# A fused LayerNorm, linear attention and SiLU MLP: reordered first loads, split first weights, deferred duplicate columns

## Chip, cores and metric

The kernel runs on one core of a Trainium2 chip. The metric is the device time of one execution in microseconds (us), as the median of several runs. The core has a matmul engine (PE, with its weight loads shown apart as PEld), three engines for other arithmetic (DVE, ACT and POOL), and SP, which here only issues DMA transfers. ACT issues a few transfers too.

## What is computed

The input x is 2048 rows of 448 numbers in bfloat16. There is one sequence; 16 heads of 28 columns; the MLP is 1792 wide.

```python
xn = _layernorm(x, axis=-1)
# linear attention
q, k, v = split((xn @ wqkv).reshape(B, S, 3, H, Dh))
pq, pk = q @ w_phi, k @ w_phi                     # per head, 28 x 28
phi_q = concat([softmax(pq), softmax(-pq)])
phi_k = concat([softmax(pk), softmax(-pk)])
kv, z = phi_k.T @ v, phi_k.sum(rows)
o = (phi_q @ kv) / (phi_q @ z + 1e-6)
# MLP
y = silu(xn @ w1) @ w2
return x + o @ wo + y
```

## The kernel before, in words

**Tiles and stages.** The rows are 16 tiles of 128; four tiles make a chunk. A contraction over 448 is cut in seven slices of 64, and nearly every matmul is issued as a pair (`pair`, L437 to L448): two matmuls of 64 rows each, one on the lower and one on the upper half of the array, each into its own PSUM bank. Two banks are a slot; slots 0 to 2 are taken and given in rotation (`take`, `give`), slot 3 is used by hand for transposes, for the fold of w_phi into w_qk, for the attention sums KV, and at the end for U.

**Head.** x is loaded by tile (`load_x`), w1 in blocks of 128 rows (`load_w1`, L510) and a last block of 64 (w16). PE first runs warm-up matmuls on a block of ones (`warm`, L488). LayerNorm of a tile is `LN_st` (statistics, L573), `LN_ag` (mean and variance, L577, variance plus epsilon into `ve`, L579, the inverse root on POOL, L581) and `LN_b` (the normalised tile xnd on DVE, L596 or L589). xnd is 512 wide: columns 448 to 511 repeat columns 0 to 63, so that every window of 128 columns can be transposed. For tiles 0 to 3 PE transposes it (`X_tr`, L459), and ACT and DVE copy the result to xT (`X_ev`, L464 and L631); for later tiles a DMA transposes (`X_dma`, L612). `F1ph` forms xn @ w1 for 128 or 256 rows, in two phases `ph` (which half of the array works on which bank) and by blocks b of w1; its `six` part uses the last 64 rows of w1. The functions `f1a`, the F1A and F1B loops and `c0` run it for chunk 0, as data arrives; `F1silu` writes silu to hT.

**Fold.** q @ w_phi is one product with a folded weight. w_qk's 448 rows are loaded in four parts to wraw; `FT_tr` transposes them on PE (L459, copies at L867), and `FM` multiplies by BD, a block diagonal of w_phi, into wqk (copies at L886). `V` forms values, `QK` scores and their exponentials; DVE sums them (L706), POOL scales (L713), a DMA transposes (phT). `F2_early` forms hT @ w2 of tiles 0 to 7 into Ye, while `KV` sums phi_k.T @ v.

**Tail.** For tiles 8 to 15 `ph0` and `ph1` form hT @ w2 in a slot seeded with x by ACT. `U(t)` forms the attention output of two tiles, DVE scales it (L800, L801, L809), and a DMA transposes it to oT (L811). `WO(t)` multiplies oT by w_o for tiles 0 to 7 and DVE adds Ye (L833); `WO_two` does the same for tiles 8 to 15 on top of the slot that already holds x and the MLP. `store` sends two tiles out (L816). `nextu` calls U ahead of its use.

**Order.** `_Prog` records every operation with a planned duration and its dependencies. PE runs them in the order of recording, and so do operations marked `ordered`, on their engine. The others are ordered by a planner (`_pass`, L239), which prices each operation by a constant and DMA by `service` (L473) and picks by due time, with shaken repeats. `chained` loads (L506) are issued only when the load four places earlier in `chain` has landed. SP issues in one line: a transfer that waits holds back all that stand behind it.

Of the kernel before, what the change touches and what calls it, by code (L numbers as in the profile page):

```python
# [140 lines left out]
class _Prog:  # L141
# [97 lines left out]
    def _pass(self, when, shake=0):  # L239
# [46 lines left out]
        while done < n:  # L286
# [20 lines left out]
            if o.is_dma:  # L307
                issue_end = t + o.dur
                eng_free[o.eng] = issue_end
                if o.fixed is not None:  # L310
                    o.end = t + o.fixed
                else:
                    x0 = max(issue_end + 900.0, dma_free[0])
                    dma_free[0] = x0 + o.nbytes
                    o.end = dma_free[0] + 300.0 + o.late
# [14 lines left out]
def bass_parallel_sum__linear_kernel_hedgehog__dense_activation_silu__prompt_kernel(  # L330
# [21 lines left out]
    with es:  # L352
# [23 lines left out]
        st6 = sb("st6", [128, NT, 6], F32)  # L376
        mv = sb("mv", [128, NT, 2], F32)
        ve = sb("ve", [128, NT], F32)
# [8 lines left out]
        wsrc = hT[:, NH - 1, FT - 1, :]  # L387
        ones_bf = wsrc[:, 0:128]
# [84 lines left out]
        def service(nbytes, run):  # L473
            return nbytes / run * (12.0 + 0.0475 * run) / 16.0
# [10 lines left out]
        P.op("pool", 230, lambda e: e.memset(wsrc, 1.0), [], [wsrc], name="ones", ordered=True)  # L485
        P.op("pool", 290, lambda e: e.affine_select(ident[:], ones_bf, [[1, 128]], ALU.is_equal, 0.0, base=0,
                                                    channel_multiplier=-1), [ones_bf], [ident[:]], name="ident", ordered=True)
        def warm(n, sl=2, d=216.0):  # L488
            for i in range(n):
                pair([(bank(2 * sl + q)[:, 0:512], ones_bf[HALF[q], :], wsrc[HALF[q], :], True, True) for q in range(2)],  # L490
                     512, "warm", dur=d)

        P.unit = "warm"
        warm(10, d=427.0)


# [13 lines left out]
        def load_w1(b, eng):  # L510
            chain.append(load(w1_sb[:, 2 * b:2 * b + 2, :].rearrange("p h f -> p (h f)"), B_w1[b * 128:(b + 1) * 128, :],
                              128 * FF * 2, 2 * FF, f"w1{b}", eng=eng, issue=480))
# [4 lines left out]
        load_x(1, 2, eng="act")  # L517
        load_w1(0, "sp")
        load_w1(1, "act")
        load_x(2, 3, eng="act")  # L520
        load_w1(2, "sp")
        for q, eng in enumerate(("sp", "act")):
            chain.append(load(w1_sb[HALF[q], 6, :], B_w1[384:448, q * 896:(q + 1) * 896], 64 * 896 * 2, 1792, f"w16{q}", eng=eng,
                              issue=480))
        load_x(3, 4, eng="act")
        P.op("pool", 300, lambda e: e.memset(BD[:], 0.0), [], [BD[:]], name="bd0", ordered=True)
# [6 lines left out]
        def load_bulk():  # L533
# [6 lines left out]
            for b in range(NB):  # L540
                r = 128 if b < 3 else 64
                chained(700.0, wraw[0:r, b, 8:904], A_wqkv[b * 128:b * 128 + r, 0:896], r * 1792, 1792, f"wqk{b}", issue=450)
# [9 lines left out]
        for q in range(2):  # L552
            for l in range(2):
                p0 = (64 if q else 8) + l * DH
                load(BD[p0:p0 + DH, :, l * DH:(l + 1) * DH], wpv[q, l], DH * NB * DH * 2, DH * 2, f"wphi{q}{l}", issue=430)

# [4 lines left out]
        def pads_init():  # L561
            for sl in range(NE):
                pads = E[:, sl].rearrange("p k (c n) -> p (k c) n", n=64)[:, :, 56:64]
                P.op("pool", 330, lambda e, pads=pads: e.memset(pads, 0.0), [], [pads], name="pads", ordered=True)
# [5 lines left out]
        def LN_st(t, od=False):  # L570
            P.unit = f"LN{t}"
            xs = x_sb[:, t, :]
            P.op("dve", 630, lambda e: e.bn_stats(st6[:, t, :], xs), [xs], [st6[:, t, :]], name="bnst", ordered=od)  # L573

        def LN_ag(t, od=False):
            P.unit = f"LN{t}"
            P.op("dve", 180, lambda e: e.bn_aggr(mv[:, t, :], st6[:, t, :]), [st6[:, t, :]], [mv[:, t, :]], name="bnag", ordered=od)  # L577
            P.op("dve" if od else "pool", 120 if od else 220,
                 lambda e: e.tensor_scalar(ve[:, t:t + 1], mv[:, t, 1:2], EPS_LN, None, ALU.add),  # L579
                 [mv[:, t, 1:2]], [ve[:, t:t + 1]], name="ve", ordered=od)  # L580
            P.op("pool", 580, lambda e: e.tensor_tensor(rstd[:, t:t + 1], ve[:, t:t + 1], neghalf[:], ALU.pow),  # L581
                 [ve[:, t:t + 1], neghalf[:]], [rstd[:, t:t + 1]], name="rstd", ordered=od)

        def LN_b(t, parts=((0, D), (D, 512)), od=False):
# [7 lines left out]
            for a, b in parts:  # L592
                dst = xnd[:, t % NX, a:b]
                src = x_sb[:, t, 0:64] if a == D else x_sb[:, t, a:b]
                P.op("dve", 90 + 0.72 * (b - a),
# [19 lines left out]
        def X_tr(t, sl, ws):  # L615
            P.unit = f"X{t}"
            for k, w in enumerate(ws):
                tpair([(bank16(2 * sl + q)[:, k * 64:(k + 1) * 64], xnd[HALF[q], t % NX, w * 64:w * 64 + 128],
                        ident[HALF[q], q * 64:(q + 1) * 64]) for q in range(2)], 64, "xT_tr")

        def X_ev(t, sl, ws, both=False):
# [3 lines left out]
            for q in (1, 0):  # L625
                src = bank16(2 * sl + q)[:, 0:n * 64].rearrange("p (s n) -> p s n", s=n)
                dst = xT[:, 0, ws[0]:ws[-1] + 1:ws.step, j * 128 + q * 64:j * 128 + (q + 1) * 64]
                if q == 0 and not both:
# [20 lines left out]
        def X_rest():  # L649
            P.unit = "Xrest"  # L650
            ws = range(1, 4, 2)
            for t in range(2):
                for k, w in enumerate(ws):
                    tpair([(bank16(6 + q)[:, (2 * t + k) * 64:(2 * t + k + 1) * 64], xnd[HALF[q], t % NX, w * 64:w * 64 + 128],
                            ident[HALF[q], q * 64:(q + 1) * 64]) for q in range(2)], 64, "xT_tr")
            for q in range(2):
                src = bank16(6 + q)[:, 0:256].rearrange("p (t w n) -> p w t n", t=2, w=2)
                dst = xT[:, 0, 1:4:2, 0:256].rearrange("p w (t r n) -> p w t r n", t=2, r=2)[:, :, :, q]
                dve(lambda e, dst=dst, src=src: e.tensor_copy(dst, src), 66 + 46 * 4, [src], [dst], "xT_ev")
# [114 lines left out]
        def F2_ph(t, sl, ph, a, b, mid=None, at=3):  # L774
# [44 lines left out]
        def WO_mm(t, ub, sl, a, b, seeded):  # L819
            P.unit = f"WO{t}"  # L820
            for s in range(NS):
                op = pair([(bank(2 * sl + q)[:, a:b], oT[HALF[q], ub, s, :], wo_sb[HALF[q], s, a:b], (not seeded) and s == 0, s == NS - 1)
                           for q in range(2)], b - a, "wo")
                swapped(op, (2 * sl, 2 * sl + 1), 0)

        def WO(t, ub):
            sl = take()
            WO_mm(t, ub, sl, 0, D, False)
            for q in range(2):
                bk = bank(2 * sl + q)[:, 0:D]  # L830
                y = Ye[:, (t + q) % NYE, :]
# [381 lines left out]
```

## Time and profile before

| | |
|---|---|
| Median of 13 runs | 149.57 us (149.03 to 151.97) |
| Profiled execution: its own time | 149.03 us |
| Profiled execution: span from first to last instruction | 147.3 us |
| PE busy | 142.3 us |
| DVE, ACT, POOL busy | 92.2, 88.9, 76.3 us |
| Warm-up matmuls start | 1.40 us |
| First transposes of x | 5.64 us |
| First matmul with w1 | 6.42 us |
| First matmul of V(2) | 19.86 us |
| First matmul of chunk 1 (F1) | 33.41 us |
| Last WO_two starts | 142.98 us |

Times in the profile count from the first instruction. A row of the timeline gives start, duration, engine, source line, operation, output and inputs, shapes and count, and in brackets how long the engine had been idle and what ended the wait. A line can be that of a helper: L446 is every matmul pair, L459 every transpose on PE, L464 every ACT operation, L477 every load. The chain that ended last is followed backwards from the last instruction through whatever released each step.

### The profile page before, as it was taken

What the parts mean: (1) busy time and instruction counts of PE and PEld (TensorE: products, weight loads), DVE (VectorE), ACT (ScalarE), POOL (GpSimd) and SP (SyncE); (2) the same over time, 40 slices, a digit from 0 to 9 for tenths busy, and PEclk for the clock granted to TensorE, in tenths of its full rate; (3) what the DMA queues carried; (4) which work ended last, traced back from release to release, by engine and by line L of the source; (5) the groups of instructions that cost most, each with busy time, mean ns of one, the idle gap of its engine ahead of it and who ended that gap; (6) DMA issues with size and microseconds to landing.
All of it is one profiled execution on the core that took longest, in us unless ns stands there. A gap on an engine that the chain in (4) does not pass through costs nothing.

```text
span 147.3 us, 5049 instructions
## 1 busy us (share of the span) xinstructions
PE 142.3 (97%) x2188; PEld 87.6 (59%) x2188; DVE 92.2 (63%) x176; ACT 88.9 (60%) x119; POOL 76.3 (52%) x87
## 2 busy tenths in 40 slices
PE   6999999999999999999999999999999999999982
PEld 2589965554556555555555556655555555557861
DVE  1977379999986496841077997871158154457532
ACT  4248789898768785975987758598592022040401
POOL 3326025059999959899123999999970000000000
PEclk9999999999999999999999999999999999999999
DMA  5997989975920895369850051333769406224592
GB/s 131 387 264 162 289 250 260 119 156 162 181 55 6 168 176 122 89 145 166 179 116 0 0 123 24 71 80 69 85 134 92 100 4 187 67 77 120 145 141 89
DMA packets 44110, 19.11 MB, mean 130 GB/s; under 512 B 37240, under 2 KB 43448, under 8 KB 44088
## 3 DMA queue, kind: packets, MB, share of 16 engines
q1 hardware_dynamic: 43432, 17.87, 58.6%
q10 hardware_dynamic: 656, 0.92, 1.8%
q8 instruction: 17, 0.28, 0.9%
q14 instruction: 5, 0.04, 0.1%
HBM read 8.17 MB, written 1.84 MB: 68 GB/s over the span
## 4 chain that ended last, share of the span: by engine, by line
PE 93%; DMA 3%; DVE 1%; POOL 0%; issue 0%; ACT 0%; SPq 0%; POOLq 0%
PE psum L446 92%; DMA E<-E 3%; PE psum L459 1%; DVE E L809 1%; POOL hT L485 0%; DVE x_sb L843 0%; ACT xT L464 0%; POOL neghalf L484 0%; SPq L1153 0%; POOLq L1198 0%
## 5 line engine op out<-in xcount | busy, mean ns | idle before, releaser
L713 POOL TENSOR_TENSOR E<-E,Rk 128x896 bf16<-128x896 bf16 x32 | 53.3, 1700 | 7.0 <-DVE Rk L708 5.3
L446 PE MATMUL psum<-xT,w_sb 64*128 64x512 bf16 (+2 forms) x522 | 46.8, 324 | 0.3 <-ACT xT L464 0.3
L446 PE MATMUL psum<-w_sb,hT 64*128 64x448 bf16 (+1 forms) x504 | 45.3, 328 | 0.0
L446 PEld LDWEIGHTS psum<-w_sb,hT 64*128 64x128 bf16 x504 | 25.6, 94 | 16.4 <-ACT psum L464 0.2
L706 DVE TENSOR_REDUCE Sk<-E 128x64 f32<-128x1792 bf16 x16 | 31.9, 2004 | 2.9 <-ACT E L464 2.9
L464 ACT ACTIVATE hT<-psum 128x1024 bf16<-128x1024 f32 (+1 forms) x29 | 28.0, 992 | 8.8 <-PE psum L446 8.5
L446 PEld LDWEIGHTS psum<-xT,w_sb 64*128 64x128 bf16 x522 | 25.0, 94 | 13.9 <-issue 0.4
L464 ACT ACTIVATE E<-psum 128x896 bf16<-128x896 f32 x32 | 27.4, 916 | 6.4 <-PE psum L446 5.2
L446 PE MATMUL psum<-wqk,xT 64*128 64x448 bf16 x224 | 23.6, 349 | 0.0
L446 PEld LDWEIGHTS psum<-wqk,xT 64*128 64x128 bf16 x224 | 12.2, 94 | 8.6
L464 ACT ACTIVATE psum<-x_sb 128x448 f32<-128x448 bf16 (+1 forms) x10 | 4.6, 468 | 20.0 <-PE psum L446 19.4
L581 POOL TENSOR_TENSOR rstd<-ve,neghalf 128x1 f32<-128x1 f32 x16 | 9.1, 571 | 7.7 <-DVE ve L579 6.9
L765 POOL TENSOR_TENSOR Ye<-Ye,x_sb 128x448 f32<-128x448 f32 x8 | 8.2, 1038 | 8.8 <-DVE Ye L763 8.8
L446 PE MATMUL psum<-wo_sb,E 64*128 64x448 bf16 (+1 forms) x126 | 11.9, 328 | 0.5 <-DMA E<-E 0.5
L446 PE MATMUL psum<-wv_sb,xT 64*128 64x448 bf16 x112 | 12.0, 349 | 0.0
L589 DVE TENSOR_SCALAR xnd<-x_sb,mv,rstd 128x896 bf16<-128x896 bf16 x12 | 8.2, 722 | 5.9 <-POOL rstd L581 5.9
L573 DVE BATCH_NORM_STATS2 st<-x_sb 128x6 f32<-128x448 bf16 x16 | 9.5, 604 | 3.7 <-DMA x_sb<-in_A_x_dram 3.6
L763 DVE TENSOR_TENSOR Ye<-psum,Ye 128x448 f32<-128x448 f32 x8 | 5.0, 621 | 10.3 <-ACT Ye L464 10.2
L833 DVE TENSOR_TENSOR x_sb<-psum,Ye 128x448 bf16<-128x448 f32 x8 | 4.8, 606 | 9.7 <-PE psum L446 6.8
L809 DVE TENSOR_TENSOR E<-psum,rden 128x224 bf16<-128x224 f32 x32 | 10.2, 382 | 0.2
L446 PEld LDWEIGHTS psum<-wo_sb,E 64*128 64x128 bf16 x126 | 5.8, 94 | 4.3 <-DMA E<-E 0.8
L464 ACT ACTIVATE x_sb<-psum 128x448 bf16<-128x448 f32 (+1 forms) x8 | 3.9, 494 | 7.4 <-PE psum L446 7.4
(48 smaller groups left out, 101.8 us busy)
## 6 DMA issues: line engine op xcount, KB each, us to landing
w_sb<-in_B_w_dram SPq DMA_DIRECT2D x4, 448.0 KB, 5.2
out_dram<-x_sb SPq DMA_DIRECT2D x7, 224.0 KB, 2.1
w_sb<-in_B_w_dram SPq DMA_DIRECT2D x4, 336.0 KB, 5.6
x_sb<-in_A_x_dram SPq DMA_DIRECT2D x2, 448.0 KB, 4.8
wv_sb<-in_A_wqkv_dram SPq DMA_DIRECT2D x2, 392.0 KB, 5.4
wo_sb<-in_A_wo_dram SPq DMA_DIRECT2D x14, 56.0 KB, 2.3
phT<-in_A_wqkv_dram SPq DMA_DIRECT2D x3, 224.0 KB, 4.1
w_sb<-in_B_w_dram ACTq DMA_DIRECT2D x1, 448.0 KB, 4.9
```

Of the source, the lines that this page charges most:

```text
L446: ins = e.matmul(dst, lhsT, rhs, start=st, stop=sp, skip_group_check=True)
L459: ins = e.transpose(dst, src, idn)
L464: return P.op("act", d_act(n), lambda e: e.activation(dst, src, func, scale=scale), reads=reads or [src], writes=writes or [dst], table=ta ...
L573: P.op("dve", 630, lambda e: e.bn_stats(st6[:, t, :], xs), [xs], [st6[:, t, :]], name="bnst", ordered=od)
L581: P.op("pool", 580, lambda e: e.tensor_tensor(rstd[:, t:t + 1], ve[:, t:t + 1], neghalf[:], ALU.pow), [ve[:, t:t + 1], neghalf[:]], [rstd[ ...
L589: dve(lambda e: e.tensor_scalar(dst, src, mv[:, t, 0:1], rstd[:, t:t + 1], ALU.subtract, ALU.mult), 734, [src, mv[:, t, 0:1], rstd[:, t:t ...
L706: dve(lambda e: e.tensor_reduce(Sk[:, t % 3, :].rearrange("p (h g) -> p h g", g=2), Er, AXL.X, ALU.add), d_dve(1792), [Er], [Sk[:, t % 3, ...
L713: pool(lambda e, Eh=Eh, Rb=Rb: e.tensor_tensor(Eh, Eh, Rb, ALU.mult), 1770, [Eh, Rh], [Eh], "phi%d" % qk)
L763: dve(lambda e: e.tensor_tensor(y, b, y, ALU.add), d_dve(D), [b, y], [y], "ye_d")
L765: pool(lambda e: e.tensor_tensor(y, y, x_sb[:, t, :], ALU.add), 1110, [y, x_sb[:, t, :]], [y], "ye_x")
L809: dve(lambda e, dst=dst, src=src, rb=rb: e.tensor_tensor(dst, src, rb, ALU.mult), d_dve(224), [src, r], [dst], "o")
L833: dve(lambda e, bk=bk, y=y, dst=dst: e.tensor_tensor(dst, bk, y, ALU.add), d_dve(D), [bk, y], [dst], "out")
```

## The change

It is one edit of many small parts.

- **First loads.** x0 and x1 go first, both on SP. w1's first block is split: columns 0 to 511 of both halves are loaded from ACT once POOL has cleared BD, columns 512 to 895 later. x2 and x3 are one transfer on ACT. The four small w_phi loads move from SP's front to behind the four w_qk loads, waiting for the first of these.
- **LayerNorm.** The `ve` operation goes. The statistics get a third group of three values that holds epsilon, so the variance comes out with epsilon in it.
- **Warm-up.** The ones are 128 columns set by DVE, read four times over; nine pairs instead of ten.
- **Duplicates.** Columns 448 to 511 of xnd for tiles 0 and 1 are first set to zero and filled later; `X_rest` then redoes window 6, too.
- **Head order.** `six` parts come after the third block; part 6 of F1 runs on 512 columns for one silu; c0(0, 0) is two halves; tile 3's copy is in two parts; the copy of tile 1's second part is all on ACT; X_rest, FT_tr and FM use slots in rotation, and slot 3 joins the rotation until phase 0 ends. V(0) comes before FM(3) and FM(2), V(2) after. POOL's pad memsets wait for a PE mark.
- **Tail.** `WO` is seeded with Ye by ACT, and its result copied out by ACT and DVE. U(6) runs inside `F2_ph(12, ..)`, U(14) inside `WO(4)` after its fourth pair; the default place of a unit inside `F2_ph` is after pair 6 instead of 3.
- **Planner constants** for DMA.

```diff
-        P.op("pool", 230, lambda e: e.memset(wsrc, 1.0), [], [wsrc], name="ones", ordered=True)
+        P.op("dve", 100, lambda e: e.memset(ones_bf, 1.0), [], [ones_bf], name="ones", ordered=True)
...
+        zero = P.op("pool", 300, lambda e: e.memset(BD[:], 0.0), [], [BD[:]], name="bd0", ordered=True)
+        P.op("pool", 100, lambda e: e.memset(xnd[:, 0:2, D:512], 0.0), [], [xnd[:, 0:2, D:512]], name="xz", ordered=True)
+        P.op("dve", 90, lambda e: e.memset(st6[:, :, 6:9], 0.0), [], [st6[:, :, 6:9]], name="eps0", ordered=True)
+        P.op("dve", 90, lambda e: e.memset(st6[:, :, 8:9], D * EPS_LN), [], [st6[:, :, 8:9]], name="eps", ordered=True)
-        warm(10, d=427.0)
+        warm(9, d=427.0)
...
         load_x(0, 1)
-        load_x(1, 2, eng="act")
-        load_w1(0, "sp")
-        load_w1(1, "act")
-        load_x(2, 3, eng="act")
-        load_w1(2, "sp")
+        load_x(1, 2)
+        load_w1(0, 0, 512, "act", after=zero)
+        load_w1(1, 0, 896, "sp")
+        load_x(2, 4, eng="act")
+        load_w1(2, 0, 896, "sp")
+        load_w1(0, 512, 384, "act")
...
-        load_x(3, 4, eng="act")
...
+            for q in range(2):
+                for l in range(2):
+                    p0 = (64 if q else 8) + l * DH
+                    load(BD[p0:p0 + DH, :, l * DH:(l + 1) * DH], wpv[q, l], DH * NB * DH * 2, DH * 2, f"wphi{q}{l}", issue=430,
+                         after=chain[-4]).late = 2500.0
...
-            P.op("dve" if od else "pool", 120 if od else 220,
-                 lambda e: e.tensor_scalar(ve[:, t:t + 1], mv[:, t, 1:2], EPS_LN, None, ALU.add),
-                 [mv[:, t, 1:2]], [ve[:, t:t + 1]], name="ve", ordered=od)
...
-        LN_b(0, ((0, 256), (256, D), (D, 512)), True)
+        LN_b(0, ((0, 256), (256, D)), True)
...
+        for t in range(2):
+            LN_b(t, ((D, 512),))
...
+        for name, k in (("U0", 0), ("X3", 0), ("U1", 1), ("A", 1), ("60", 0), ("B", 0), ("X", 1), ("61", 0), ("T0", 0),
+                            ("01", 0), ("20", 0), ("M0", 0), ("21", 0), ("40", 1), ("M1", 0), ("T1", 0), ("41", 0), ("V0", 0),
+                            ("M3", 1), ("M2", 0), ("V2", 0)):
+            if k:
+                free.insert(0, free.pop(k))
+            head[name]()
...
+            for q in range(2):
+                act(bank(2 * sl + q)[:, 0:D], Ye[:, (t + q) % NYE, :], ACTF.Identity, D, name="seed")
+            WO_mm(t, ub, sl, 0, D, mid)
...
-                dve(lambda e, bk=bk, y=y, dst=dst: e.tensor_tensor(dst, bk, y, ALU.add), d_dve(D), [bk, y], [dst], "out")
+                if q:
+                    dve(lambda e, bk=bk, dst=dst: e.tensor_copy(dst, bk), d_dve(D), [bk], [dst], "out")
+                else:
+                    act(dst, bk, ACTF.Identity, D, name="out")
...
-        ph1(12, 0, D)
-        nextu(6)
+        F2_ph(12, sls[12, 0], 1, 0, D, lambda: nextu(6), 8)
         ph0(14, 0, M)
-        wo2(4, 12)
+        WO(4, ub[4], lambda: nextu(14))
+        WO_two(12, ub[12], sls[12, 0], 0, D)
```

In the list of the head, U0 and U1 are the two phases of part 6 of F1 on tiles 0 and 1, 60 and 61 those on tiles 2 and 3, X3 the transposes of tile 3, A and B the halves of c0(0, 0), X is X_rest, T0 and T1 are FT_tr, M0 to M3 FM, V0 and V2 the values, and the other pairs of digits c0(part, phase).

## The prediction, on record before the result

> **What bounds the kernel now.** I read the page's busy times and its chain first, then the waits of the matmul engine (PE), then the timeline at the three places where PE stops.
>
> ```profile
> span 147.3 us, 5049 instructions
> PE 142.3 (97%) x2188; PEld 87.6 (59%) x2188; DVE 92.2 (63%) x176; ACT 88.9 (60%) x119; POOL 76.3 (52%) x87
> ...
> PE 93%; DMA 3%; DVE 1%; POOL 0%; issue 0%; ACT 0%; SPq 0%; POOLq 0%
> ```
>
> ```profile
> engine line waited for: us in total, times, longest us
> PE psum L446 <- POOL hT L485: 1.4, 1, 1.4
> PE psum L446 <- DMA E<-E: 0.5, 1, 0.5
> PE psum L446 <- ACT xT L464: 0.3, 1, 0.3
> ```
>
> PE is the bound and hardly waits: only the stretch before its first useful matmul, one short wait behind it, and one 0.5 us wait near the end can be won. Its rows run at one pitch, so moving matmuls about inside the stream is worth nothing. The head, from the timeline:
>
> ```profile
> 1.40 4.45 PE L446 MATMUL psum<-hT 64*128 64x512 bf16 x20 [1.40 <-POOL hT L485]
> ...
> 3.85 0.18 DVE L577 BATCH_NORM_AGGREGATE mv<-st 128x2 f32<-128x6 f32 x1
> 4.06 0.15 DVE L579 TENSOR_SCALAR ve<-mv 128x1 f32<-128x1 f32 x1
> 4.13 0.62 DVE L573 BATCH_NORM_STATS2 st<-x_sb 128x6 f32<-128x448 bf16 x1
> ...
> 5.07 0.79 DVE L596 TENSOR_SCALAR xnd<-x_sb,mv,rstd 128x256 bf16<-128x256 bf16 x3
> ...
> 5.64 0.52 PE L459 MATMUL psum<-ident,xnd 64*128 64x64 bf16 x10
> ...
> 6.42 0.55 PE L446 MATMUL psum<-xT,w_sb 64*128 64x128 bf16 x8 [0.26 <-ACT xT L464]
> ```
>
> The x20 row is warm-up on ones; useful work starts at 5.64 with the transposes of tile 0. The tail, from the chain in order of time:
>
> ```profile
> 137.48 0.90 DVE E L809 x3
> 138.38 0.02 SPq L1153
> 138.40 0.03 issue
> 138.43 4.50 DMA E<-E
> 142.94 0.05 issue
> 142.98 1.53 PE psum L446 x28
> ```
>
> The last attention unit, U(14), is scaled by DVE, transposed by a DMA that takes 4.50 us here (2.7 is the median of the eight), and only then can the last output product WO_two(14) run.
>
> [...] ten warm-up pairs fill 1.40 to about 5.64, 0.425 us a pair, where a pair of that width later takes 0.216; the first four f1 pairs start over 0.37 us (6.42 to 6.79), the next eight over 0.46 (6.87 to 7.33). [...] ve, one element a partition, takes 0.15 us. [...] the two w1 transfers issued at 1.25 (SP) and 1.35 (ACT) land 4.3 and 4.9 us later.
>
> **The change part by part**, against the profiled run (149.03 us, span 147.3, 1.7 around it); the median of 13 is 149.57, 0.54 more, and I carry the difference over unchanged.
>
> *Start of the stream.* Each ve (L579) stretches the DVE chain: aggregate to next instruction is 0.28 (3.85 to 4.13) and 0.29 (4.78 to 5.07), of which the aggregate is 0.18; with epsilon folded into a third statistics group both go, 2 x 0.10 = 0.20. The aggregate then reads 9 values, not 6: taken as free. rstd for tile 0 could start at about 4.1 instead of 4.30, so it doesn't bind. x0 (landed 2.4 us after 0.79) no longer shares with x1: 0 to 0.2 sooner, 0.1 taken. x1 comes second on SP, at about 1.2 instead of 0.92: with 2.6 to land, 3.8, needed at about 3.9. So xn0 moves from 5.07 to about 4.77 and the weight load of the first transpose, 0.46 behind it today (5.53), to 5.24. The warm-up must be out of the way: its ones come from a DVE memset of 128 columns instead of POOL's 0.53 us one, so it starts near 0.95 and nine pairs end near 4.8. The new DVE memsets run while DVE is idle (to 3.19). First transpose 5.64 to 5.24: **gain 0.40**, 0.25 to 0.5. Deferring the 64-column duplicates (0.31 each) takes them off DVE ahead of xT's copies; on PE it only helps hold that 0.40. w1's first part must be there by 6.0: it waits on ACT for BD's memset (near 1.6), and the first w1 transfer today lands 4.3 after issue, with more bytes: 5.9 at worst. Queued behind that wait on ACT are x2/x3, the rest of w1 and the first copies, none due before 5.5. Rows 2 of w1 land at 1.71 + 6.1 = 7.8 today and are due at 8.59, then about 8.25; rows 6 land near 8.9, due at about 9.1 before and after, since the six-blocks are put behind. x3's 112 KB now stand ahead of them where w_phi's 24 KB stood behind: cover 0.2 to 0.4, all of it needed; a slip of 0.3 would cost 0.1 to 0.3 of the 0.40. x2 and x3 in one transfer feed only DVE, which waits for x2 until 8.36 with its transposes due at 11.23.
>
> *Clock.* Useful work now begins 0.4 earlier. If the clock rises at the same moment (about 6.8, where the pitch of f1 pairs falls from 0.093 to 0.057), 0.4 us more of it runs at half speed and 0.20 is lost; if the rise moves with the warm-up, nothing. I take **-0.10**.
>
> *More instructions.* c0(0,0) in two halves: 16 pairs of 128 columns at 0.056 (the 0.46 over eight above) for 8 of 256 at 0.109 (48 matmuls, 24 pairs, from 8.59 to 11.23): +0.02. Two more pairs of transposes at 0.03: +0.06. **-0.08**.
>
> *Order in the head.* Two small stops lie there. At 13.28 PE waits for ACT's 0.55 us copy of tile 3 (12.59): the 16 transpose pairs before it start by 13.06, 0.19 goes. Its copy becomes a 4-window and a 3-window one with U1 and half A ahead of the reader; counting 0.32 to ACT's start, 0.38 + 0.33 for the copies and 0.14 back against 0.8 + 0.22 of PE work, about 0.14 remains. At 19.73 X_rest waits for DVE on the one slot 3 (0.17); it gets a slot in rotation. **+0.20**, 0 to 0.35. T0 moves some 1.8 us later, so wqk is safe.
>
> *w_phi behind w_qk.* Four issues (0.43 to 0.60 each, 2.07 in all) leave SP's front and stand ahead of w_v, behind the landing of wqk0 (6.26 + 4.0 = 10.3). w_v's first issue goes from 10.31 to about 12, its second from 12.07 to 12.6; everything on SP behind them moves as much. Today the second lands at 12.07 + 6.5 = 18.5; V(0) in the new order is reached at about 19.2. In idle DMA time the delay vanishes; undiluted, wv1 lands at 19.1 to 19.7. Taken **-0.10**, 0 to -0.6. w_phi itself is due at FM0, about 16, and lands by 14.5.
>
> *Elsewhere.* POOL loses twelve ve's (2.6 us) and its pad memsets wait for PE, with rstd of tiles 4 to 7 behind them, due at 22: nothing. Planner constants reorder SP: the last xT transpose for chunk 1 lands at 29.25 + 3.0 = 32.3, its reader is at 33.41; cover 1.1 us, so 0.
>
> *Tail.* nextu(14) moves into WO(4), three of its seven pairs earlier; a 448-column pair takes 0.189 (QK's 14 pairs from 22.82 to the next row at 25.47), so 0.57. On DVE one 0.56 copy stands before U(14)'s products where two additions stood around; the products still begin some 1.4 us after U(14). Need comes 0.57 later relative to supply. The wait is 142.98 less 142.32 (14 f2 pairs from 140.98 at 0.096), 0.66; at 4.5 us of DMA 0.09 stays. **+0.57**, 0.4 to 0.66. Added: WO's banks are seeded from Ye by ACT (2 x 0.54) before its first matmul; ACT is 2.7 us busy in 130 to 140. Worst is WO(6): 0.23 to the evictions of WO_two(12), two of 0.54, two seeds of 0.54, 2.4 us against 28 pairs of 0.096 (136.97 to 139.65) = 2.7. Covered by 0.3; lost if those evictions slip.
>
> Sum: 0.40 - 0.10 - 0.08 + 0.20 - 0.10 + 0.57 = 0.89. 149.03 becomes 148.14, the median 149.57 becomes **148.7**.
>
> **Rivals.** [...] PE now idles from about 4.8 to 5.24 and again to 6.0, and small transposes fill it badly. [...] 3.4 us at half speed costs 1.7: 149.57 - 0.89 + 1.7 = 150.4, slower. [...] For it: the gap doubles. Against it: the warm-up starts 0.45 sooner. *The weights arrive late.* V(0) waits the full 0.6 for w_v: 149.2, no change. For it: wv1 lands only 0.7 before V(0) even undelayed. Against it: DMA moves only 162 GB/s in the slice from 11 to 14.7, against 387 in the second slice, so there is room to catch up. *The tail doesn't shrink,* the transpose taking longer beside earlier stores: 149.57 - 0.32 = 149.25, no change. Against it: 2.7 us is usual.
>
> **How the numbers follow.** About 0.5% (0.75 us) is what this measurement can tell from none: under 148.82 is faster. Forecast 0.60, own range 148.1 to 149.1 (0.52 faster, 0.08 within); late weights 0.12 (within); tail 0.07 (within); clock 0.21 (0.20 slower, 0.01 within). So 0.52, 0.28, 0.20. The range reaches from best gains (148.1) to the clock case's middle (150.4).
>
> **What would show it.** Right: first transpose near 5.2, f1 near 6.0, no PE wait on DMA E at the end, useful matmuls at full pitch by 7. Wrong: f1 pairs of 0.107 us beyond 7.5 (clock), a PE wait on wv_sb near 19, or on w_sb between 8 and 10.

## The result and the profile after

The changed kernel is slower: 153.26 us in the median of 11 runs (150.37 to 155.93), against 149.66 us of the kernel before in 48 runs (148.32 to 152.15). The medians stand 2.4% apart. The ratio of the comparison is 1.0131 with a 95% interval of 1.0075 to 1.0187; it leaves out every execution more than 1.5% above its kernel's fastest, and of the changed kernel that keeps only two, so the medians say more here. Medians and ratio both say slower. The forecast was 148.7 us.

The profiled execution took 153.32 us, its span is 151.6. The page shows PE still as the bound, with more busy time and more waiting:

```profile
span 151.6 us, 5108 instructions
PE 143.9 (95%) x2206; PEld 119.3 (79%) x2206; DVE 89.9 (59%) x174; ACT 94.8 (63%) x131; POOL 73.1 (48%) x75
...
PE 92%; DMA 4%; issue 1%; ACT 1%; DVE 0%
```

The chain now holds 4% of DMA and 1% of "issue". PE's waits by releaser (total, times, longest) name them:

```profile
PE psum L444 <- DMA w_sb<-in_B_w_dram: 2.8, 1, 2.8
PE psum L444 <- DVE st L493: 1.1, 1, 1.1
PE psum L444 <- issue: 1.0, 1, 1.0
```

The 1.1 us is the start of the warm-up, which began at 1.40 before. The waits for DMA E at the end and for ACT's xT are gone. New are 2.8 us for w1 and 1.0 us for which the profile has no releaser. The head in the timeline (start, duration, engine, line, operation):

```profile
1.12 4.02 PE L444 MATMUL psum<-hT 64*128 64x512 bf16 x18 [1.12 <-DVE st L493]
...
1.70 0.64 ACTq L475 DMA_DIRECT2D w_sb<-in_B_w_dram  x1
1.73 1.51 SPq L475 DMA_DIRECT2D w_sb<-in_B_w_dram  x3
...
4.96 0.58 PE L457 MATMUL psum<-ident,xnd 64*128 64x64 bf16 x10
...
8.30 0.61 PE L444 MATMUL psum<-xT,w_sb 64*128 64x128 bf16 x8 [2.76 <-DMA w_sb<-in_B_w_dram]
...
8.82 1.04 PE L444 MATMUL psum<-xT,w_sb 64*128 64x128 bf16 x16
```

and the same x16 row in the kernel before:

```profile
6.87 0.62 PE L446 MATMUL psum<-xT,w_sb 64*128 64x128 bf16 x16
```

The transposes start at 4.96, earlier than the forecast's 5.24. But w1's first part, issued by ACT at 1.70, lands at 8.25, and f1 starts at 8.30 where it started at 6.42 before. And f1 then runs at half speed: the eight pairs of the x16 row stand 0.107 us apart, and the 256-column pairs 0.213 us, up to 13.0. Before, full speed came at 6.8, and the x16 row took 0.62 us. The chain shows the third piece:

```profile
1.70 6.56 DMA w_sb<-in_B_w_dram
...
19.02 2.63 PE psum L444 x59
21.66 1.03 issue
22.69 1.05 PE psum L444 x25
...
24.20 124.60 PE psum L444 x1761
148.80 0.02 issue
```

From 24.20 to the end PE runs without a stop. So the whole loss lies ahead of 24 us. The pieces add up, span against span. Work at half speed is counted as half lost, and the 0.08 is the forecast's own figure, so that the sum is exact is in part chance.

| Piece | us |
|---|---|
| f1 starts at 8.30, not 6.42 | +1.88 |
| half speed from 8.30 to 12.99, half of it lost (2.35), against 6.42 to 6.78 before (0.18) | +2.17 |
| stop inside one matmul pair, 21.39 to 22.69, less the pair's own 0.11 | +1.19 |
| two more transpose pairs, 128-column pairs (from the forecast) | +0.08 |
| the two stops of before at 13.28 and 19.73 are gone (0.19, 0.17) | -0.36 |
| PE's wait at the end is gone | -0.66 |
| sum | +4.30 |
| measured, 151.6 less 147.3 | +4.3 |

The theory from this: three losses, each with its own cause, namely late first weights, a clock kept low by the wait for them, and a stop of PE that comes from no data at all. Rivals: the new order of the head loses time by itself; the clock would have stayed low even with the weights in time; the stop at 21.7 is chance or bound to that place in the work.

### The profile page after: what moved, and what is told of

The parts are those of the page before. It is cut to its first block, busy times and chain, and to the rows that moved or that the text cites. A ratio compares the mean times of both kernels' runs of the same rounds, so it can differ in the third digit from the quotient of the medians.

```text
span 151.6 us, 5108 instructions
## 1 busy us (share of the span) xinstructions
PE 143.9 (95%) x2206; PEld 119.3 (79%) x2206; DVE 89.9 (59%) x174; ACT 94.8 (63%) x131; POOL 73.1 (48%) x75
## 4 chain that ended last, share of the span: by engine, by line
PE 92%; DMA 4%; issue 1%; ACT 1%; DVE 0%
PE psum L444 91%; DMA w_sb<-in_B_w_dram 4%; PE psum L457 1%; ACT L517 1%; DVE x_sb L853 0%
## 5 line engine op out<-in xcount | busy, mean ns | idle before, releaser
L444 PE MATMUL psum<-xT,w_sb 64*128 64x512 bf16 (+2 forms) x538 | 50.0, 332 | 3.8 <-DMA w_sb<-in_B_w_dram 2.8
L444 PEld LDWEIGHTS psum<-xT,w_sb 64*128 64x128 bf16 x538 | 35.1, 101 | 10.3 <-DMA w_sb<-in_B_w_dram 2.9
L444 PEld LDWEIGHTS psum<-w_sb,hT 64*128 64x128 bf16 x504 | 34.7, 94 | 7.6
L462 ACT ACTIVATE hT<-psum 128x1024 bf16<-128x1024 f32 x28 | 28.3, 1022 | 11.4 <-PE psum L444 10.5
L444 PEld LDWEIGHTS psum<-wqk,xT 64*128 64x128 bf16 x224 | 18.6, 94 | 2.5 <-issue 0.3
L581 POOL TENSOR_TENSOR rstd<-mv,neghalf 128x1 f32<-128x1 f32 x16 | 8.7, 561 | 20.6 <-DVE mv L580 20.6
L462 ACT ACTIVATE x_sb<-psum 128x448 bf16<-128x448 f32 (+1 forms) x12 | 5.8, 512 | 19.2 <-PE psum L444 13.8
L444 PEld LDWEIGHTS psum<-wv_sb,xT 64*128 64x128 bf16 x112 | 9.6, 94 | 0.5
L444 PEld LDWEIGHTS psum<-wo_sb,E 64*128 64x128 bf16 x126 | 7.3, 94 | 2.4
L444 PEld LDWEIGHTS psum<-vb,E 64*128 64x128 bf16 x256 | 8.1, 94 | 0.8
```

The lines of the kernel that those rows point to most:

```text
L444: ins = e.matmul(dst, lhsT, rhs, start=st, stop=sp, skip_group_check=True)
L462: return P.op("act", d_act(n), lambda e: e.activation(dst, src, func, scale=scale), reads=reads or [src], writes=writes or [dst], table=ta ...
```

## The experiments

Fourteen kernels, each timed beside the kernel before on the same chip. PE's order is the same as in the parent kernel, apart from the edit; in some of them the planner moves a few later instructions of SP and DVE by some places.

### The first weights: place in the queues, or form of the transfer?

**The first part on SP.**

```diff
-        load_w1(0, 0, 512, "act", after=zero)
+        load_w1(0, 0, 512, "sp")
```

> The changed kernel with one edit: w1's first part is issued by SP directly behind x1, ahead of rows 1 and 2, and waits for nothing. Theory Q (its place in the queues makes it late): it is issued near 1.7 and lands by 6.0, as the first w1 transfer of the kernel before lands 4.3 us after its issue; PE idles under 0.6 us before f1 instead of 2.76, the half-speed pairs (0.107 us at 128 columns) end by 9; time 149.2 (148.6 to 150.4) instead of 153.3. Rival S (two parts of 1 KB pieces are slow by themselves): the part lands after 7.5, f1 starts after 7.5, time 152 or more. Rival C (the clock is lost to the gap between warm-up and f1 even without late weights): f1 starts near 6, but pairs of 0.107 last to 10 or beyond, time 150.4 to 151.2.

Measured: 153.85 us (4 runs, 153.51 to 154.83). Theory Q fell. f1 starts at 7.97 and stops again:

```profile
7.97 0.61 PE L444 MATMUL psum<-xT,w_sb 64*128 64x128 bf16 x8 [2.10 <-DMA w_sb<-in_B_w_dram]
...
9.36 0.93 PE L444 MATMUL psum<-xT,w_sb 64*128 64x128 bf16 x14 [0.56 <-DMA w_sb<-in_B_w_dram]
```

The edit also did something I had not meant: with nothing to wait for, ACT issued x2 and x3 at 0.93 and w1's second part at 1.36, ahead of SP's first part at 1.73. So this run speaks against "its place alone", but it isn't clean: the part stood behind other loads again.

**One block at the same place.**

```diff
-        load_w1(0, 0, 512, "act", after=zero)
+        load_w1(0, 0, 896, "act", after=zero)
...
-        load_w1(0, 512, 384, "act")
```

> The changed kernel with one edit: w1's first rows go as one whole block again (128 pieces of 3.5 KB), at the same place on ACT behind the same wait; the second part is dropped. Theory Q: the place is unchanged and the bytes are 75% more, so it lands no earlier than 8.2 and f1 starts at 8.3 or later; time 153.3 to 154.5. Rival S (the split form is what is slow): it lands by 6.5, PE idles under 1 us, time near 149.5.

Measured: 151.24 us (14 runs, 149.71 to 153.19). Rival S holds for the landing: three quarters more bytes arrive 1.8 us earlier. The time is above its 149.5: in the profiled execution full speed comes only at 9.72, and a stop of 0.6 us is left at 18.9.

```profile
6.49 0.61 PE L444 MATMUL psum<-xT,w_sb 64*128 64x128 bf16 x8 [0.93 <-DMA w_sb<-in_B_w_dram]
```

The packets of the two traces suggest why. ACT's issue of the split part takes 0.64 us and ends at 2.34, behind SP's issue of rows 1 (to 2.15); its first 1 KB packet moves at 4.61, when nearly all of rows 1 is through. The one block takes 0.39 us to issue, ends at 2.09, ahead of SP, and 82 of its 128 packets start between 2.7 and 4.5. So the split part starts later; how much that alone costs, no run shows.

**Rows 2 held back.** In the changed kernel 9 of the part's 16 completions come by 5.91, the other 7 between 6.58 and 8.25.

```diff
-        load_w1(2, 0, 896, "sp")
+        load_w1(2, 0, 896, "sp", after=chain[0])
```

> The changed kernel with one edit: SP issues rows 2 of w1 only when w1's first part has landed; the part stays split (1 KB pieces) and on ACT. In the changed kernel's trace 9 of the 16 completions of that part come by 5.91 and the other 7 between 6.58 and 8.25, while pieces of 3.5 KB of rows 2 pass. Theory M (small pieces fall behind large ones [...]): without rows 2 beside it the part lands by 6.2 to 6.6, f1 starts by 6.7, 1.7 us of the wait go and part of the half-speed stretch; rows 2 then land near 9, just in time; time 150.5 (149.8 to 152.3). Rival D (small pieces are slow whatever stands beside them, their issue of 0.64 us too): still 7.5 or later, time 153 or more.

Measured: 150.57 us (4 runs, 150.37 to 151.49). Theory M holds. The part, still split, lands at 6.12 instead of 8.25, though its first packet moves as late as before (4.54). So rows 2 beside it cost these 2.1 us. Now rows 2 are late instead:

```profile
6.16 0.40 PE L444 MATMUL psum<-xT,w_sb 64*128 64x128 bf16 x8 [0.69 <-DMA w_sb<-in_B_w_dram]
...
9.48 1.72 PE L444 MATMUL psum<-xT,w_sb 64*128 64x256 bf16 x28 [1.08 <-DMA w_sb<-in_B_w_dram]
```

In the changed kernel 93 packets of 3.5 KB from SP and 30 of 1 KB from ACT start between 5.5 and 6.5: in this microsecond the large ones moved some 326 KB and the small ones some 30 KB. By what order the two kinds are served is not shown, since the packet records do not name the engine.

### The clock

**The wait filled.** Nine more warm-up pairs between the transposes and f1, in the changed kernel:

```diff
+        P.unit = "warm"
+        warm(9, sa[0])
         f1a(0, 0, 0)
```

> The changed kernel with nine more warm-up pairs between the first transposes and f1, to fill PE's 2.76 us of waiting; the weights come as late as before this edit. Theory W (the wait costs twice: once itself, once by keeping the clock low to 13.0): f1 still starts at 8.3 to 8.6 but its 128-column pairs take 0.057 from the start or soon after; 4.6 us at half speed shrink to under 1.2, so about 1.8 to 2.3 us are won back: 151.2 (150.8 to 152). Rival F (the rate rises at its own moment whatever PE does): pairs of 0.107 until about 13, time 153.3 to 153.8.

Measured: 151.30 us (4 runs, 151.17 to 151.62), 2.0 less than the changed kernel, with the weights as late as ever. Theory W holds:

```profile
5.58 2.63 PE L444 MATMUL psum<-hT 64*128 64x512 bf16 x18
8.05 0.39 PE L444 MATMUL psum<-xT,w_sb 64*128 64x128 bf16 x8
...
8.39 0.62 PE L444 MATMUL psum<-xT,w_sb 64*128 64x128 bf16 x16
```

The same 16 matmuls take 0.62 us, not 1.04. The trace's clock record has full speed from 6.66 on, not from 12.99. So about half of what the late weights cost in the profiled execution, they cost through the clock.

How short a gap is enough? The kernel before with a shorter warm-up and nothing else:

```diff
-        warm(10, d=427.0)
+        warm(8, d=427.0)
```

> The kernel before with one edit: 8 warm-up pairs instead of 10, so that PE stands idle for 0.85 us ahead of its first transpose, about as long in all as the changed kernel would with its weights in time; nothing that follows starts later for it. Theory K (a gap of 0.9 to 1.1 us ahead of f1 lets the clock rise a step of 3.41 us later in about half of the executions, at up to 1.7 us each): median 150.4 (149.9 to 151.2), single times from 148.5 to 152. Rival V (such a gap is not enough to keep the clock down): 149.4 to 149.8 with the spread of the kernel before.

Measured: 150.53 us (14 runs, 148.69 to 151.77), beside 149.42 us of the kernel before. The single times fall in two groups: six from 148.69 to 149.63, eight from 150.51 to 151.77. Theory K holds in the profile: that execution (150.80) is of the second group, its clock record has full speed from 9.79, not 6.78, and half of these 3.0 us, 1.5, is lost. It has a stop of 0.8 us at 19.3 as well (of the kind told below), so the distance of the groups, some 1.9 us, is not the clock's alone.

```profile
1.40 3.59 PE L446 MATMUL psum<-hT 64*128 64x512 bf16 x16 [1.40 <-POOL hT L485]
5.45 0.59 PE L459 MATMUL psum<-ident,xnd 64*128 64x64 bf16 x10 [0.46 <-DVE xnd L596]
6.15 0.61 PE L446 MATMUL psum<-xT,w_sb 64*128 64x128 bf16 x8
...
6.66 1.06 PE L446 MATMUL psum<-xT,w_sb 64*128 64x128 bf16 x16
```

The x16 row takes 1.06 us, half speed again. Matmuls end near 4.8 and begin again at 6.15, with ten small transposes between. The step of the clock is in the traces too: with the loads of the changed kernel in the kernel before (next run) it is full from 4.18 to 7.60, half to 11.01, then full: 3.41 us each. An estimate from that trace and the changed kernel's: counted back from the changed kernel's rise at 12.99, steps of that length would run from 2.75 to 6.16, 6.16 to 9.58 and 9.58 to 12.99. In the first PE has no matmul but transposes for the last 1.2 us, in the second it stands idle for 2.1 us, and behind the third, in which it is busy for all of the 3.41 us, the clock rose. That PE's work in such a step decides is not shown beyond that. The moment of the rise differs between executions. With rows 2 held back, f1 at 6.16 and for 1.2 us ahead of it transposes alone, the clock rose at 5.95; with one block, f1 at 6.49 and 1.5 us, at 9.72. So with a wait of 0.93 us for the weights the clock was low for 3.2 us of f1 in that profile. With the old loads in the changed kernel (below), full speed is there at 5.20 in the one profile; that the clock rises in time in every execution, once the weights do, isn't shown.

The granted clock of the single executions fits this. In the next run's profile one step at half speed after a first rise makes it 0.989. Eight of the changed kernel's twelve executions, the profiled one counted in, have 0.987 to 0.989, but only two of the 119 of the kernel before that were timed beside the experiments, and none of the four with the wait filled.

**Are the loads alone the cause?** The kernel before with the head's loads of the changed kernel:

```diff
-        load_x(1, 2, eng="act")
-        load_w1(0, "sp")
-        load_w1(1, "act")
-        load_x(2, 3, eng="act")
-        load_w1(2, "sp")
+        load_x(1, 2)
+        load_w1(0, 0, 512, "act", after=zero)
+        load_w1(1, 0, 896, "sp")
+        load_x(2, 4, eng="act")
+        load_w1(2, 0, 896, "sp")
+        load_w1(0, 512, 384, "act")
```

> The kernel before with only the loads at the head taken from the changed kernel (x0 and x1 on SP, w1's first part on ACT behind the memset of BD, x2 and x3 as one, w1's second part behind them); order of work, statistics, w_phi and tail as in the kernel before. Theory Q: f1 starts at 8 to 8.5 and half speed lasts to 10 or beyond, so 1.7 to 2.0 plus 1.0 to 2.2 us are lost: 152.5 to 153.8 instead of 149.6. Rival O (the loss needs the new order of the head or the later stop at 21.7): 149.4 to 151.

Measured: 151.27 us (4 runs, 150.68 to 151.79). The loads alone make the kernel before slower by 1.7 us, between the two forecasts: the part lands at 7.37, not 8.25. Its profile has a stop of 0.7 us at 20.5 as well, of the kind told below, so not all of the 1.7 need be the wait and the clock.

```profile
7.41 0.48 PE L446 MATMUL psum<-xT,w_sb 64*128 64x128 bf16 x8 [1.55 <-DMA w_sb<-in_B_w_dram]
```

More than half of the changed kernel's loss is left for something else.

**The block on SP, in the changed kernel.**

```diff
-        load_w1(0, 0, 512, "act", after=zero)
-        load_w1(1, 0, 896, "sp")
+        load_w1(0, 0, 896, "sp")
+        load_w1(1, 0, 896, "act", after=zero)
...
-        load_w1(0, 512, 384, "act")
```

> The changed kernel with w1's first rows as one block (128 pieces of 3.5 KB) on SP behind x1, rows 1 on ACT in its place behind the wait for BD's memset, then x2 and x3; the second part is dropped. The one-block run before it had f1 at 6.49 and lost 0.8 us in one stop at 18.9. Theory P (PE waits in three places: weights, clock, its own instructions): the block lands near 5.7, f1 starts near 5.9, PE waits under 0.6; the half-speed pairs end by 7 to 10; a stop of 0 to 1 us with no releaser stays near 18; time 149.3 (148.3 to 150.8). Rival O (the new order of the head costs by itself): f1 early and time still above 151.

Measured: 151.73 us (4 runs, 149.67 to 152.70), above my 149.3. The profiled execution is the 149.67 one, with the clock up at 5.46; even so PE waits 1.2 us for the block (rows 1 move beside it and land at 6.19, the block at 6.63), 0.5 us for rows 2 (landed 9.27), and 0.4 us without a releaser at 18.4. f1 starts at 6.68, not near 5.9, so rival O is neither shown nor refuted by it.

**All first loads as before.** The changed kernel with `load_x` and `load_w1` calls of the kernel before (the diff above, the other way round); the rest stays changed.

> The changed kernel with all loads of x0 to x3 and w1 as in the kernel before (one block first, x1 and rows 1 on ACT, x2 and x3 apart); statistics, order of the head, w_phi behind w_qk and tail stay changed. Theory P (what the change loses, it loses through the late first weights): w1's first block lands near 5.6, f1 starts by 6.0, no PE wait on w_sb over 0.4, half speed ends by 8.3 whichever moment the clock takes; up to 0.6 us may still go in the stop near 18. Time 148.6 (147.8 to 149.6). Rival O (something else in the head or behind it costs as well): 150 or more.

Measured: 151.65 us (6 runs, 150.16 to 153.08). By my own numbers rival O is right. No wait on w_sb is left, and full speed is there at 5.20; yet the stop without a releaser has grown. The profiled execution is the fastest of the six, at 150.16; what the others lose beyond it isn't seen, but three of them have a granted clock of 0.989.

```profile
16.57 1.04 PE L444 MATMUL psum<-xT,w_sb 64*128 64x256 bf16 x15
19.55 0.92 PE L444 MATMUL psum<-xT,w_sb 64*128 64x256 bf16 x13 [1.93 <-issue]
```

Fifteen matmuls are an odd number: PE stops in the middle of a pair, where no semaphore wait stands.

### The stop: PE waits for its own instructions

I counted PE's records in each trace (weight loads, matmuls and semaphore waits, in order of time). Wherever the stop occurs, in 12 traces of different kernels, PE stops after the same number of them: 705 (two later traces stop after the 961st, 256 on). The DMA queue q8, "instruction" on the page, moves 17 packets of 16 KB in the changed kernel beside 4467 such records, one for about every 263; that a packet is 256 of PE's instructions is my estimate from this and from the 256 between the two stops. The second of these packets, called the second fetch here, starts at the 470th to 513th record in the four traces without a stop at the 705th, 192 to 235 ahead of it; where it starts later, PE stops there. The table counts from the 449th, 256 ahead of the 705th; when a fetch is asked for, no trace shows. The second fetch of each profile (times in us):

| Kernel | PE passes its 449th | fetch starts | ends | PE at its 705th | goes on |
|---|---|---|---|---|---|
| before | 12.89 | 14.02 | 15.60 | 18.08 | at once |
| changed | 17.32 | 19.93 | 21.30 | 21.39 | 22.69 |
| changed, old loads | 13.28 | 16.68 | 18.02 | 17.34 | 19.55 |
| before, new tail (below) | 12.58 | 15.57 | 16.89 | 17.77 | 18.17 |
| changed, w_v held (below) | 18.37 | 19.13 | 20.33 | 22.44 | at once |
| changed, old loads, 36 pairs (below) | 11.10 | 11.71 | 12.84 | 14.88 | at once |

PE goes on 1.3 to 1.6 us after a late fetch has ended. In the changed kernel two things make a late fetch dear: what moves while it is due (next run), and that the new order runs those 256 instructions in 4.07 us where the old one takes 5.2, because it puts the small transposes and fold products of X_rest, T0 and M0 close together. The new order is not needed for a stop: kernels with the old one stop as well, for 0.4 to 1.2 us. And how late the fetch comes isn't fixed: the kernel before and the one with the new tail run the same PE instructions up to there, and their fetches start 1.1 and 3.0 us after the 449th; why, the traces don't show.

**w_v held back.** The w_v transfers and all behind them in SP's line are moved to a function called ahead of X_rest:

```diff
+                P.ops[-1].deps.add(mk.id)
...
+            if name == "X":
+                load_rest(mark())
             head[name]()
```

> The changed kernel with one edit: the two w_v transfers, and all that SP issues behind them, wait until PE has passed the 256-column f1 pairs before X_rest (about 17.8), some 3 us later than 14.92. Theory I (the stop at 21.66 is PE waiting for its next 16 KB of instructions, whose transfer stands behind w_v's 896 B pieces): the fetch that started at 19.93 now starts by 18.6, the stop of 1.0 to 1.3 us near 21.5 is gone; w_v lands near 22.5 to 23.5, V(0) at about 23.4 waits 0 to 0.6; time 152.4 (151.9 to 153.2) with the weights and the clock as late as in the changed kernel. Rival R (the stop has another cause): it stays, time 153.3 to 154.

Measured: 152.40 us (4 runs, 151.05 to 154.95). The agreement of the time is partly luck: the stop goes, but PE waits 1.7 us for w_v, not 0 to 0.6. The profiled execution is the slowest of the four, so only its order of events is used. The fetch starts 0.76 us after the 449th instruction instead of 2.6, and the 28 matmuls at which the changed kernel stopped run through (timeline):

```profile
21.66 1.70 PE L444 MATMUL psum<-xT,w_sb 64*128 64x256 bf16 x28
```

and in PE's waits:

```profile
PE psum L444 <- DMA wv_sb<-in_A_wqkv_dram: 1.7, 1, 1.7
```

The edit also holds back what SP issues behind w_v: SP issues in one line, and in the changed kernel nothing left it from 3.24 to 7.96, while a load waited 4.7 us for w1. But in the changed kernel nearly all that moves between 17.0 and 19.9, while the fetch is due, are packets of 896 bytes (813 of 837), the size of w_v's (448 in each of the two transfers). So w_v's packets are what holds the fetch there; how they hold it is not shown.

**The count shifted.** The warm-up in narrow pairs, in the kernel with old loads:

```diff
-        warm(9, d=427.0)
+        warm(36, d=107.0)
```

(and `warm` issues pairs of 128 columns)

> The kernel of the run before (changed kernel with the loads of before, 151.65, stop of 1.93 us at 17.34 in its profile) with one edit: the warm-up is 36 pairs of 128 columns instead of 9 of 512, the same time at half speed, 108 more PE instructions ahead of everything. Theory I (PE stops at its 705th instruction because the 16 KB fetch [...] stands behind w_v's pieces: [...] 16.68 served, 19.55 resumed): the 449th instruction is now reached near 11, ahead of w_v's burst, the fetch is served within 1.2 us, and no stop of more than 0.4 us is left between 12 and 25; time 149.6 (148.2 to 150.6). Rival R (the stop is bound to the place in the work, not to the count of instructions): it stays near 17.3, time 151 to 152.

Measured: 150.50 us (22 runs, 148.88 to 152.45), 1.15 less. Theory I holds: the same work runs through at the old place, though it stood near 17.3 with a 1.93 us stop a run earlier.

```profile
16.40 1.70 PE L444 MATMUL psum<-xT,w_sb 64*128 64x256 bf16 x28
...
33.90 3.41 PE L444 MATMUL psum<-xT,w_sb 64*128 64x512 bf16 x30 [0.59 <-issue]
```

The second line is a new stop. PE reaches chunk 1 about 5 us earlier than in the changed kernel (32.94 against 38.26), and the last of the four DMA transposes that make its xT, issued at 28.9, takes some 5 us. Start to start PE loses 0.8. The forecast had given that transfer 1.1 us of cover. In the changed kernel it is issued at 33.9, takes at most 4.2 us, and is in time for the later PE. A smaller stop of 0.5 us comes at PE's 961st instruction, 256 on.

**Are the remaining spread and the last us the clock?** In that kernel PE still stops for 0.36, 0.10 and 0.45 us ahead of f1.

```diff
-        warm(36, d=107.0)
+        warm(39, d=107.0)
...
+        warm(4, sa[0], d=107.0)
         f1a(0, 0, 0)
```

> The kernel of the run with old loads and 36 warm-up pairs (150.5, single times from 148.88 to 152.45), with PE's gaps before f1 filled: 39 warm-up pairs of 128 columns and four more between the first transposes and f1; in that run's profile PE had stopped for 0.36, 0.10 and 0.45 us between 4.8 and 5.85. Theory K (in most executions the clock rises one 3.41 us step later [...]): the single times close up, most of them below 150; median 149.5 (148.7 to 150.0). Rival V (the spread has another cause: instruction fetches, late rows of w1): median 150.2 to 151, times up to 152 as before.

Measured: 150.46 us (22 runs, 149.34 to 152.95): nothing gained. Theory K fell for this rest, and rival V stands. With the clock up from 4.20 the profiled execution waits 0.5 us for rows 1 at 6.2 and loses 1.1 at PE's 961st instruction and 0.9 at the start of chunk 1.

### The tail and the statistics alone

**The tail in the kernel before** (the change's `WO`, `WO_mm`, the places of U(6) and U(14), `at=6`):

> The kernel before with only the tail of the change: U(14) inside WO(4), U(6) inside the second half of F2(12), WO's banks seeded on ACT, its two evictions shared by ACT and DVE. Theory T (the tail part is worth what the wait on E shows): the 0.5 to 0.66 us wait of PE for the last DMA transpose is gone, time 149.0 (148.8 to 149.3) instead of 149.6. Rival U (seeding and evictions put something else in its place): a wait on ACT or DVE at 138 to 141, time 149.6 or more.

Measured: 148.74 us (10 runs, 148.25 to 150.33), beside 149.63; ratio 0.9965, interval 0.9920 to 1.0009. PE has no wait left behind 20 us:

```profile
20.04 123.78 PE psum L446 x1796
143.82 0.02 issue
143.84 0.39 DVE x_sb L850
```

Theory T holds in the trace. The gain of 0.89 in the medians isn't shown to be more than noise, as the interval just reaches 1.

**The statistics added to it** (epsilon as a third group, no `ve`, narrow ones from DVE):

> The kernel before with the tail of the change (that alone was 148.74 beside 149.63) and, added, only its statistics: epsilon as a third group of statistics, no ve instructions, ones of 128 columns from DVE, ten warm-up pairs. Loads, order of the head and w_phi are those of before. Theory S: the first transposes move from 5.64 to about 5.4 (ten pairs from 1.1 end there) and f1 waits for w1 at 5.5 to 5.6 or starts by 6.2; 0.2 us won: 148.5 (148.0 to 149.0). Rival N (the start is bound by x or by the weights, not by the statistics): 148.7 to 149.3.

Measured: 149.15 us (14 runs, 148.50 to 150.05), beside 149.36. By the time it is rival N: nothing is won. But in the profile the start is earlier, as theory S has it: the first transposes come at 5.28, f1 at 6.09, just after w1's block has landed (6.05). Then the fetch starts 3.9 us after the 449th instruction, and PE stops for 1.0 us at the 705th. So the profile shows an earlier start that the stop takes back; it doesn't show that the statistics gain nothing.

**The tail with a narrow warm-up**, 40 pairs of 128 for 10 of 512, as a try at the best version:

> The kernel before with the tail of the change (148.74 beside 149.63) and its warm-up as 40 pairs of 128 columns instead of 10 of 512: 120 more PE instructions in the same time. In that run's profile the stop at the 705th instruction was 0.3 to 0.4 us. Theory I: the stop and with it the slower executions go: 148.3 (147.9 to 148.7). Rival N (nothing, or a stop at another place, because the instruction fetches only meet another transfer): 148.7 to 149.3.

Measured: 151.00 us (14 runs, 148.64 to 154.00). Both theories fell short. Rows 1 are 1.1 us late in its profile (15 of 16 completions by 5.90, the last at 8.05), which brings PE to its 449th instruction at 12.48, back in the burst, and it stops for 0.8 us at the 705th. So the shift of the count, which won 1.15 us in the kernel with old loads, won nothing here. No version was shown to beat the kernel before; the new tail alone is the one that may.

## Why the prediction was wrong

- **Start of the stream (+0.40): wrong, and this is the step that failed.** The transposes came at 4.96, better than 5.24. But "w1's first part must be there by 6.0: ... the first w1 transfer today lands 4.3 after issue, with more bytes: 5.9 at worst" took the time of a whole block as an upper bound for a part of it. The part landed 6.56 us after issue: it is twice as many pieces, which are dearer to issue (0.64 against 0.39 us), started 2.9 us after issue, behind rows 1, and fell behind the larger packets of rows 2. Cost: f1 started 1.88 later than before, where 0.40 earlier was forecast. The rows-held run shows the larger cause, 2.1 us for standing beside rows 2; the part of the late start is read from the packets alone.
- **Clock (-0.10): wrong by size, 2.17.** The rival, that the clock rises later, was priced at 1.7. That price is about right: half of a step of 3.41 us, as the clock record of the kernel before with the changed loads has them, is 1.7, and the 8-pair run, with a gap of 1.35 us, loses 1.5 to the clock in its profile. Its sign, f1 pairs of 0.107 us beyond 7.5, came true. But it was treated as a case by itself at 0.21. A late transfer and a late clock come together: the wait is what makes the gap, and it kept the clock low for 4.7 us of f1 (to 12.99; with the gap filled it rose at 6.66).
- **Not in the sum at all: the instruction stop, 1.19.** "Its rows run at one pitch, so moving matmuls about inside the stream is worth nothing" is the sentence that hid it. The order sets how long 256 instructions last (4.07 us, 5.2 in the old one), and w_v's packets held up their fetch (2.6 us behind the 449th, 0.76 with w_v held back). The kernels with the old order stop, too, so the order isn't the cause by itself.
- **Extra instructions (-0.08) and order of the head (+0.20):** both small stops of before are gone, about 0.36, so the order is right in direction; the 0.08 wasn't measured apart.
- **w_phi behind w_qk (-0.10):** no PE wait on w_v in the changed kernel, nor in the 36-pair run, where V(0) starts at 19.20 as forecast. The feared wait didn't come; what w_v delayed was the fetch.
- **Elsewhere (0):** the xT transpose for chunk 1 did not cost anything, because PE came late; with the old loads and the count shifted it costs 0.8 (the 36-pair run). The cover of 1.1 was counted in PE's old time.
- **Tail (+0.57): right in the trace.** The wait of 0.66 is gone in the changed kernel; alone the tail gave 0.89 in the medians, with an interval that reaches 1.
- **The range** ended at 150.4, the middle of one rival; two losses that come together, and one unknown, lay beyond it.

What stays open: how much of the single executions' spread (150.4 to 155.9) is the clock's moment and how much the fetch; each is shown, their shares per execution are not, as only the profiled executions left a trace. Why the fetch is late in one trace and not in another with the same instructions is open, too. Whether an order that spaces the small matmuls out would avoid the stop wasn't tried.

## What to carry to other kernels

Price a split transfer by its pieces and by what else moves beside it, not by its bytes: a small part, sent "first" in small pieces, landed later here than one large transfer in its place (6.56 us from issue against 4.75). Where PE starts, count a late load twice, once as a wait and once as the clock that stays low behind it (1.88 and 2.17 us here). When a stop has no releaser and falls inside a pair, count the engine's instructions: if it falls on the same count in kernel after kernel (the 705th in 12 of 16 traces here), the engine may be waiting for its own code.

## What was unexpected of the hardware

- PE stopped after its 705th instruction in 12 of the 16 traces, for 0.4 to 2.2 us. In these its 16 KB fetch had started 1.9 to 3.9 us after the 449th, in the other four 0.6 to 1.1 us; it went on 1.3 to 1.6 us after the fetch ended.
- 256 KB in 1 KB pieces took 6.56 us from issue to landing beside rows 2 in 3.5 KB pieces, 4.42 us with rows 2 held back, and 448 KB in 3.5 KB pieces 4.75 us at the same place.
- In the profiled execution of the 8-pair run PE had a gap of about 1.35 us without matmuls ahead of f1, transposes in it, and half speed lasted to 9.79, where the kernel before has full speed from 6.78. In the clock record of the kernel before with the changed loads, full and half speed last 3.41 us each.
